# k'v and its product with q on halves of the TensorE array, all pieces of a batch in one slot

## The chip, the cores and the metric

One core of one Trainium2 chip. The metric is the device time of one execution, in microseconds (us). Runs of one kernel differ by a microsecond or two; so beside the times this text uses single executions taken by the profiler, stretch by stretch. PE is TensorE's matmul side, PEld its weight loads, DVE is VectorE, ACT ScalarE, POOL GpSimd, SP the engine that issues most transfers.

## The reference, cut to what matters

```python
def _attn_ref(q, k, v, g_norm):                    # (8 batches, 8 heads, 576 tokens, 64)
    kv = np.einsum('bhsd,bhse->bhde', k, v)        # 64 x 64 per head
    out = np.einsum('bhsd,bhde->bhse', q, kv)
    rms = np.sqrt(np.mean(out * out, axis=-1, keepdims=True) + 1e-06)
    return out / rms * g_norm
# then, on x = out as (4608 tokens, 512): gelu(x @ w_gate) * (x @ w_val) @ w_out,
# gated by sigmoid(x @ w_res), added to x
```

A head is 64 wide, half of the 128x128 array. Two heads side by side, a "pair", fill it. A batch has 4 x 128 tokens and a remainder of 64; the remainders of two batches share a tile of 128 rows.

Of the kernel before, what the change touches and what calls it, by code (L numbers as in the profile page):

```python
# [18 lines left out]
def kernel(  # L19
# [22 lines left out]
    NJ = 4  # L42
# [99 lines left out]
    def attn_begin(b):  # L142
        st[b] = {
            "qT": attnp.tile([P, NJ, NP, P], FP16, tag="qT", name="qT"),
            "kv2": attnp.tile([P, NP, P], FP16, tag="kv2", bufs=3, name="kv2"),
            "ss": attnp.tile([P, NJ + 1, H], FP32, tag="ss", name="ss"),
            "o": {},
        }
# [10 lines left out]
    def kv_steps(b, ps, pr):  # L159

        k16 = b16_t[b, "k"].rearrange("p j h d -> p j (h d)")
        v16 = b16_t[b, "v"]
        if b == 0:
            lasts = [[t[:, j].rearrange("p h d -> p (h d)") for t in first_last] for j in range(2)]
        else:
            lasts = [[t.rearrange("p h d -> p (h d)") for t in last_kv[b % 2]]]
        cs = slice(pr * P, (pr + 1) * P)
        for j in range(NJ):
            nc.tensor.matmul(  # L169
                ps,  # L170
                lhsT=k16[:, j, cs],
                rhs=v16[:, 2 * pr : 2 * pr + 2, j * D : (j + 1) * D],
                start=(j == 0),
                stop=False,
            )
        for i, (kl, vl) in enumerate(lasts):
            nc.tensor.matmul(ps, lhsT=kl[:, cs], rhs=vl[:, cs], start=False, stop=(i == len(lasts) - 1))  # L177

    def a_kv(b, lo, hi):
        if lo == 0:  # L180
            st[b]["kvp"] = pattn.tile([P, NP, P], FP32, tag="at", name="kvp")
        ps = st[b]["kvp"]
        for pr in range(lo, hi):
            kv_steps(b, ps[:, pr, :], pr)
        if hi == NP:
            nc.vector.tensor_tensor(
                out=st[b]["kv2"], in0=ps, in1=mask[:, None, :].to_broadcast([P, NP, P]), op=ALU.mult
            )

    def a_ss(b, j, ps):  # L190
        sq = attnp.tile([P, H, D], FP32, tag="sq", name="sq")
        nc.scalar.activation(out=sq, in_=ps, func=AF.Square)  # L192
        nc.vector.tensor_reduce(out=st[b]["ss"][:, j, :], in_=sq, op=ALU.add, axis=mybir.AxisListType.X)  # L193

    def a_o(b, j):
        s = st[b]
        ps = pattn.tile([P, C], FP32, tag="at", name="op")
        for pr in range(NP):
            nc.tensor.matmul(  # L199
                ps[:, pr * P : (pr + 1) * P], lhsT=s["qT"][:, j, pr, :], rhs=s["kv2"][:, pr, :], start=True, stop=True  # L200
            )
        a_ss(b, j, ps)
        s["o"][j] = ps

    def a_rem_o(b):
        ps = pattn.tile([P, C], FP32, tag="at", name="orp")
        for pr in range(NP):
            for e in range(2):
                nc.tensor.matmul(  # L209
                    ps[:, pr * P : (pr + 1) * P],  # L210
                    lhsT=qtr[e][:, pr, :],
                    rhs=st[2 * pair(b) + e]["kv2"][:, pr, :],
                    start=(e == 0),
                    stop=(e == 1),
                )
        o32 = attnp.tile([P, C], FP32, tag="o32", name="o32")
        nc.scalar.copy(out=o32, in_=ps)
        a_ss(b, NJ, ps)
        st[b]["o"][NJ] = o32
# [28 lines left out]
    def a_t(b, j):  # L248

        s = st[b]  # L250
        blk, jj = where(b, j)
        nc.vector.tensor_tensor(  # L252
            out=t_t[blk][:, jj, :].rearrange("p (h d) -> p h d", h=H),
# [591 lines left out]
```

## The kernel before: the parts that the change and the argument touch

The big matmuls of batch m (here "block m") run in slots of 8 matmuls of 512 columns, 1.73 us each. The attention of batch m+1 is put between the slots, in small pieces.

```python
def kv_steps(b, ps, pr):                  # k'v of one pair of heads, whole array
    ...
    cs = slice(pr * P, (pr + 1) * P)      # P = 128: two heads
    for j in range(NJ):                   # 4 token tiles, then the remainder
        nc.tensor.matmul(ps, lhsT=k16[:, j, cs], rhs=v16[:, 2*pr : 2*pr+2, j*D : (j+1)*D], ...)
    for i, (kl, vl) in enumerate(lasts):
        nc.tensor.matmul(ps, lhsT=kl[:, cs], rhs=vl[:, cs], ...)

def a_kv(b, lo, hi):
    ...                                   # two of the four blocks of a pair are of no use:
    nc.vector.tensor_tensor(out=st[b]["kv2"], in0=ps, in1=mask[...], op=ALU.mult)

def a_o(b, j):                            # product with q, one token tile
    ps = pattn.tile([P, C], FP32, tag="at", name="op")
    for pr in range(NP):
        nc.tensor.matmul(ps[:, pr*P : (pr+1)*P], lhsT=s["qT"][:, j, pr, :], rhs=s["kv2"][:, pr, :], ...)

def a_rem_o(b):                           # remainder rows of two batches
    ...  lhsT=qtr[e][:, pr, :]            # copies of qrT, each with the other batch's half zeroed

# in plan_attn(b): where the pieces stand (b == 2: k0, o0, n0 = 4, 6, 10; else 1, 3, 7)
at(m, k0, lambda: a_kv(b, 0, 2))          # half of k'v
at(m, k0 + 1, lambda: a_kv(b, 2, 4))      # the other half
at(m, o0, lambda: a_rem_o(b))             # if the batch has a remainder to do
for j in range(NJ):
    at(m, o0 + j, lambda j=j: a_o(b, j))  # four slots
```

## Time and profile before

| | before |
|---|---|
| time, median of 3 runs | 353.95 us |
| span of the profiled run | 352.1 us |
| PE busy | 343.4 us (98%) |
| DVE / ACT busy | 61% / 35% |

The page's groups by line and shape give the four groups of matmuls that the change touches. Columns: line, engine, operation, output and inputs, rows*columns of the array in use, shape of the moving tile, count; then busy time and mean ns of one; then idle time before them.

```profile
L169 PE MATMUL kvp<-v,k 128*128 128x128 f16 x128 | 11.0, 222 | 1.1 <-POOL v L535 0.8
L199 PE MATMUL op<-kv,qT 128*128 128x128 f16 x112 | 10.7, 219 | 0.0
L177 PE MATMUL kvp<-vl,kl 128*128 128x128 f16 x28 | 6.1, 219 | 0.0
L209 PE MATMUL orp<-kv,qtr 128*128 128x128 f16 x32 | 2.4, 219 | 0.0
```

They use all of the array (128*128), but half of each k'v result is thrown away by the mask, and half of what the product multiplies is zero. Do not read the cost off "mean ns": matmuls overlap in the pipeline, and what one costs is its distance to the next one's start, 0.0558 us here.

### The profile page before, as it was taken

What the parts mean: (1) busy time and instruction counts of PE and PEld (TensorE: products, weight loads), DVE (VectorE), ACT (ScalarE), POOL (GpSimd) and SP (SyncE); (2) the same over time, 40 slices, a digit from 0 to 9 for tenths busy, and PEclk for the clock granted to TensorE, in tenths of its full rate; (3) what the DMA queues carried; (4) which work ended last, traced back from release to release, by engine and by line L of the source; (5) the groups of instructions that cost most, each with busy time, mean ns of one, the idle gap of its engine ahead of it and who ended that gap; (6) DMA issues with size and microseconds to landing.
All of it is one profiled execution on the core that took longest, in us unless ns stands there. A gap on an engine that the chain in (4) does not pass through costs nothing.

```text
span 352.1 us, 5059 instructions
## 1 busy us (share of the span) xinstructions
PE 343.4 (98%) x1907; PEld 168.0 (48%) x1907; DVE 215.6 (61%) x434; ACT 124.9 (35%) x216; POOL 50.2 (14%) x79
## 2 busy tenths in 40 slices
PE   8799999999999999999999999999999999999995
PEld 3544554454454445444554455444544444444443
DVE  6855377869757765766478646855687433344433
ACT  3663534462254213522363125312642233223320
POOL 2782420150050005000320031000000000000000
PEclk9999999999999999999999999999999999999999
DMA  7999999697999079905691569037001500020013
GB/s 241 304 197 203 197 202 122 181 151 89 207 132 104 2 184 153 118 0 132 133 185 9 127 144 183 3 78 178 0 2 42 151 2 0 30 90 2 1 30 91
DMA packets 78507, 38.74 MB, mean 110 GB/s; under 512 B 42386, under 2 KB 74002, under 8 KB 78482
## 3 DMA queue, kind: packets, MB, share of 16 engines
q0 software_dynamic: 38752, 17.17, 38.9%
q1 hardware_dynamic: 39488, 21.11, 22.4%
q8 instruction: 15, 0.25, 0.3%
q10 hardware_dynamic: 242, 0.13, 0.1%
q14 instruction: 10, 0.08, 0.1%
HBM read 38.80 MB, written 9.44 MB: 137 GB/s over the span
## 4 chain that ended last, share of the span: by engine, by line
PE 91%; DMA 4%; DVE 3%; issue 0%; ACT 0%; SPq 0%; POOL 0%; DVEq 0%
PE gps L315 26%; PE vps L315 26%; PE fps L348 26%; PE rps L335 9%; PE kvp L169 2%; PE op L199 2%; DMA kf<-in_k_dram 2%; DMA vf<-in_v_dram 1%; DMA out_dram<-osb 1%; DVE t L594 1%; DVE ss L580 1%; PE orp L209 1%; PE kvp L177 0%; PE vps L620 0%; PE gps L620 0%
## 5 line engine op out<-in xcount | busy, mean ns | idle before, releaser
L304 DVE TENSOR_TENSOR hid<-ge,vps 128x512 f16<-128x512 f16 x108 | 73.3, 684 | 65.3 <-PE vps L315 58.5
L315 PE MATMUL gps<-xT,wg 128*128 128x512 f16 x424 | 108.8, 379 | 0.3 <-ACT xT L265 0.3
L315 PE MATMUL vps<-xT,wv 128*128 128x512 f16 x424 | 108.8, 379 | 0.0
L303 ACT ACTIVATE ge<-gps 128x512 f16<-128x512 f32 x108 | 64.4, 598 | 112.4 <-PE gps L315 103.3
L348 PE MATMUL fps<-wo,hid 128*128 128x512 f16 x420 | 96.7, 379 | 0.0
L315 PEld LDWEIGHTS <-wv 128*128 128x128 f16 x424 | 41.5, 98 | 50.0
L348 PEld LDWEIGHTS <-hid 128*128 128x128 f16 x420 | 40.8, 98 | 48.1
L315 PEld LDWEIGHTS <-wg 128*128 128x128 f16 x424 | 40.0, 98 | 41.8 <-issue 0.5
L354 DVE SCALAR_TENSOR_TENSOR pf<-th,fps 128x512 f32<-128x512 f32 x35 | 23.8, 687 | 47.8 <-PE fps L348 47.8
L344 ACT ACTIVATE th<-rps 128x512 f32<-128x512 f32 x36 | 21.5, 598 | 79.5 <-PE rps L335 79.5
L335 PE MATMUL rps<-wr,xT 128*128 128x512 f16 x144 | 36.5, 379 | 0.0
L193 DVE TENSOR_REDUCE ss<-sq 128x8 f32<-128x512 f32 x32 | 21.4, 683 | 6.3 <-ACT sq L192 4.6
L359 DVE SCALAR_TENSOR_TENSOR osb<-pf,t 128x512 f32<-128x512 f32 x35 | 24.2, 691 | 1.1
L335 PEld LDWEIGHTS <-xT 128*128 128x128 f16 x144 | 14.1, 98 | 17.0
L192 ACT ACTIVATE sq<-op 128x512 f32<-128x512 f32 x28 | 16.6, 598 | 9.7 <-PE op L199 9.0
L728 POOL COPY hold<-qT 1x1 f16<-1x1 f16 x5 | 0.9, 178 | 134.1 <-DMA qT<-q 134.1
L252 DVE TENSOR_TENSOR t<-op,ny 128x512 f16<-128x512 f32 x28 | 17.8, 680 | 0.1
L271 DVE TENSOR_TENSOR t<-t,g 128x512 f16<-128x512 f16 x36 | 13.3, 418 | 0.0
L169 PE MATMUL kvp<-v,k 128*128 128x128 f16 x128 | 11.0, 222 | 1.1 <-POOL v L535 0.8
L169 PEld LDWEIGHTS <-k 128*128 128x128 f16 x128 | 9.2, 100 | 5.1 <-issue 1.8
L199 PEld LDWEIGHTS <-qT 128*128 128x128 f16 x112 | 8.4, 98 | 5.5 <-issue 0.2
L199 PE MATMUL op<-kv,qT 128*128 128x128 f16 x112 | 10.7, 219 | 0.0
(107 smaller groups left out, 180.7 us busy)
## 6 DMA issues: line engine op xcount, KB each, us to landing
out_dram<-osb SPq DMA_DIRECT2D x32, 256.0 KB, 2.4
qraw<-in_q_dram POOLq DMA_DIRECT2D x7, 512.0 KB, 6.0
kraw<-in_k_dram POOLq DMA_DIRECT2D x7, 512.0 KB, 8.6
v<-in_v_dram POOLq DMA_DIRECT2D x7, 512.0 KB, 10.7
wg<-in_moe_w_gate_dram POOLq DMA_DIRECT2D x2, 512.0 KB, 8.2
wv<-in_moe_w_val_dram POOLq DMA_DIRECT2D x2, 512.0 KB, 8.9
wo<-in_moe_w_out_dram POOLq DMA_DIRECT2D x2, 512.0 KB, 14.5
out_dram<-osb SPq DMA_DIRECT2D x6, 128.0 KB, 2.3
```

The source lines that it names most:

```text
L169: nc.tensor.matmul(ps, lhsT=k16[:, j, cs], rhs=v16[:, 2 * pr : 2 * pr + 2, j * D : (j + 1) * D], start=(j == 0), stop=False,)
L193: nc.vector.tensor_reduce(out=st[b]["ss"][:, j, :], in_=sq, op=ALU.add, axis=mybir.AxisListType.X)
L199: nc.tensor.matmul(ps[:, pr * P : (pr + 1) * P], lhsT=s["qT"][:, j, pr, :], rhs=s["kv2"][:, pr, :], start=True, stop=True)
L252: nc.vector.tensor_tensor(out=t_t[blk][:, jj, :].rearrange("p (h d) -> p h d", h=H), in0=s["o"][j].rearrange("p (h d) -> p h d", h=H), in1 ...
L303: nc.scalar.activation(out=ge, in_=gps, func=AF.Gelu)
L304: nc.vector.tensor_tensor(out=hids[blk][:, f, :], in0=ge, in1=vps, op=ALU.mult)
L315: nc.tensor.matmul(ps[:, j0 * P : j1 * P], lhsT=w[:, cc, :], rhs=xT_t[blk][:, j0:j1, cc, :], start=(cc == 0 and j0 == 0), stop=(cc == NP - ...
L335: nc.tensor.matmul(rps, lhsT=xT_t[blk][:, j, cc, :], rhs=wr16[:, cc, :], start=(cc == 0), stop=(cc == NP - 1),)
L344: nc.scalar.activation(out=th, in_=rps, func=AF.Tanh, scale=0.5)
L348: nc.tensor.matmul(fps, lhsT=hids[blk][:, f, j * P : (j + 1) * P], rhs=wo16[:, f, :], start=(f == 0), stop=(f == NF - 1))
L354: nc.vector.scalar_tensor_tensor(out=pf, in0=th, scalar=1.0, in1=fps, op0=ALU.add, op1=ALU.mult)
L359: nc.vector.scalar_tensor_tensor(out=osb, in0=pf, scalar=0.5, in1=t_t[blk][:, j, :], op0=ALU.mult, op1=ALU.add)
```

## The change

The intent is to give the two heads of a pair a half of the array each. In k'v the halves are columns (64 of k as weights, output on 64 partitions), in the product they are rows (64 partitions of q' and of k'v). Neighbouring matmuls use different halves and can overlap. Since going from the whole array to halves and back costs time, all pieces of a batch stand in one slot: one visit for k'v, one for the product, one for the remainder. (A visit is a stretch of tiled matmuls between two whole-array ones.) The remainder uses quarters and goes a slot earlier; batch 0 keeps the old form. In batch 1 the normalisation and the first output transposes move a slot ahead as well. Core of the diff:

```diff
+    def a_kv(b):
+        ps = pattn.tile([P, NP, D], FP32, tag="at", name="kvp")
         for pr in range(NP):
+            for j in range(NJ + 1):
+                for e in range(2):
+                    h = 2 * pr + e
+                    nc.tensor.matmul(
+                        ps[halves(e), pr, :],
+                        lhsT=k16[:, j, h, :] if j < NJ else kl[:, h, :],
+                        rhs=v16[:, h, j * D : (j + 1) * D] if j < NJ else vl[:, h, :],
...
+        nc.vector.tensor_copy(out=st[b]["kv2"], in_=ps)
+    def a_o(b):
+        for jj in range(NJ // 2):
+            for e in range(2):
+                o[2 * jj + e] = pattn.tile([P, 2, NP, D], FP32, tag="at", name="op")
+            for j in range(2):
+                for pr in range(NP):
+                    for e in range(2):
+                        nc.tensor.matmul(
+                            o[2 * jj + e][:, j, pr, :],
+                            lhsT=st[b]["qT"][halves(e), 2 * jj + j, pr, :],
+                            rhs=kv_of(b, e, pr), ...
     def a_rem_o(b):
+                        ps[e][halves(i), pr, :],
+                        lhsT=qrT[halves(e), pr, halves(i)],
+                        rhs=kv_of(2 * pair(b) + i, e, pr), ...
...                                          # m_out_last, the last tile of the output
+        osb_all = finp.tile([P, C], FP32, tag="osb", bufs=3, name="osb")
-            osb = finp.tile([P, n], FP32, tag="osb", bufs=3, name="osb")
+            osb = osb_all[:, cs]
...                                          # opening: fillers that keep PE busy in waits
-    ... o0 rows8 vc2P ... t1 cols8 sq2 ...
+    ... o0 warm2 vc2P ... t1 warm1 sq2 ...
...                                          # plan of batch 1: x are the output transposes
-            2 * NF + 1: [x[0], x[1]],
-            2 * NF + 2: [x[2], x[3]],
+            2 * NF: [x[0], x[1]],
+            2 * NF + 1: [x[2]],
+            2 * NF + 2: [x[3]],
...                                          # plan of batches 2 to 7
-        at(m, k0, lambda: a_kv(b, 0, 2))
-        at(m, k0 + 1, lambda: a_kv(b, 2, 4))
+        at(m, k0, lambda: a_kv(b))
         if rem:
-            at(m, k0 + 1, lambda: rem_qT_copy(b))
-            at(m, o0, lambda: a_rem_o(b))
+            at(m, o0 - 1, lambda: a_rem_o(b))
+        at(m, o0, lambda: a_o(b))
```

More of the change, by code (lines that the diff above doesn't have):

```diff
@@ L144, in attn_begin @@
             "qT": attnp.tile([P, NJ, NP, P], FP16, tag="qT", name="qT"),
-            "kv2": attnp.tile([P, NP, P], FP16, tag="kv2", bufs=3, name="kv2"),
+            "kv2": (
+                attnp.tile([P, NP, D], FP16, tag="kv2", bufs=3, name="kv2")
+                if b > 0
+                else consts.tile([P, NP, P], FP16, name="kv0")
+            ),
             "ss": attnp.tile([P, NJ + 1, H], FP32, tag="ss", name="ss"),
@@ L157, in a_qT @@
         nc.scalar.copy(out=st[b]["qT"][:, 2 * jj : 2 * jj + 2, :, :], in_=ps)
-    def kv_steps(b, ps, pr):
-        k16 = b16_t[b, "k"].rearrange("p j h d -> p j (h d)")
-        v16 = b16_t[b, "v"]
-        if b == 0:
-            lasts = [[t[:, j].rearrange("p h d -> p (h d)") for t in first_last] for j in range(2)]
-        else:
-            lasts = [[t.rearrange("p h d -> p (h d)") for t in last_kv[b % 2]]]
-        cs = slice(pr * P, (pr + 1) * P)
-        for j in range(NJ):
-            nc.tensor.matmul(
-                ps,
-                lhsT=k16[:, j, cs],
-                rhs=v16[:, 2 * pr : 2 * pr + 2, j * D : (j + 1) * D],
-                start=(j == 0),
-                stop=False,
-            )
-        for i, (kl, vl) in enumerate(lasts):
-            nc.tensor.matmul(ps, lhsT=kl[:, cs], rhs=vl[:, cs], start=False, stop=(i == len(lasts) - 1))
@@ L179, in a_kv @@
-    def a_kv(b, lo, hi):
-        if lo == 0:
-            st[b]["kvp"] = pattn.tile([P, NP, P], FP32, tag="at", name="kvp")
-        ps = st[b]["kvp"]
-        for pr in range(lo, hi):
-            kv_steps(b, ps[:, pr, :], pr)
-        if hi == NP:
-            nc.vector.tensor_tensor(
-                out=st[b]["kv2"], in0=ps, in1=mask[:, None, :].to_broadcast([P, NP, P]), op=ALU.mult
-            )
-    def a_ss(b, j, ps):
-        sq = attnp.tile([P, H, D], FP32, tag="sq", name="sq")
-        nc.scalar.activation(out=sq, in_=ps, func=AF.Square)
-        nc.vector.tensor_reduce(out=st[b]["ss"][:, j, :], in_=sq, op=ALU.add, axis=mybir.AxisListType.X)
@@ L195, in a_o, with halves, kv_of @@
-    def a_o(b, j):
-        s = st[b]
-        ps = pattn.tile([P, C], FP32, tag="at", name="op")
-        for pr in range(NP):
-            nc.tensor.matmul(
-                ps[:, pr * P : (pr + 1) * P], lhsT=s["qT"][:, j, pr, :], rhs=s["kv2"][:, pr, :], start=True, stop=True
-            )
-        a_ss(b, j, ps)
-        s["o"][j] = ps
+    def halves(e):
+        return slice(e * D, (e + 1) * D)
+    def kv_of(b, e, pr):
+        kv2 = st[b]["kv2"]
+        return kv2[halves(e), pr, :] if b > 0 else kv2[halves(e), pr, halves(e)]
@@ new lines, in a_kv @@
+    def a_kv(b):
+        k16 = b16_t[b, "k"]
+        v16 = b16_t[b, "v"]
+        kl, vl = last_kv[b % 2]
+        ps = pattn.tile([P, NP, D], FP32, tag="at", name="kvp")
+        for pr in range(NP):
+            for j in range(NJ + 1):
[5 more added lines that the diff above has]
+                        rhs=v16[:, h, j * D : (j + 1) * D] if j < NJ else vl[:, h, :],
+                        start=(j == 0),
+                        stop=(j == NJ),
+                    )
+        nc.vector.tensor_copy(out=st[b]["kv2"], in_=ps)
@@ new lines, in a_o @@
+    def a_o(b):
+        o = st[b]["o"]
+        for jj in range(NJ // 2):
[7 more added lines that the diff above has]
+                            lhsT=st[b]["qT"][halves(e), 2 * jj + j, pr, :],
+                            rhs=kv_of(b, e, pr),
+                            start=True,
+                            stop=True,
+                        )
@@ new lines, in of_o, with a_ss @@
+    def of_o(ap, i):
+        jj, e = i // 2, i % 2
+        return ap[:, 2 * jj : 2 * jj + 2].rearrange("p j (r e) -> p j r e", e=2)[:, :, :, e]
+    def a_ss(b, i):
+        o, ss = st[b]["o"][i], st[b]["ss"]
+        sq = attnp.tile([P, 2, NP, D] if i < NJ else [P, H, D], FP32, tag="sq", name="sq")
+        src = o if i < NJ else o.rearrange("p (h d) -> p h d", h=H)
+        nc.scalar.activation(out=sq, in_=src, func=AF.Square)
+        out_ = of_o(ss, i) if i < NJ else ss[:, NJ, :]
+        nc.vector.tensor_reduce(out=out_, in_=sq, op=ALU.add, axis=mybir.AxisListType.X)
@@ L205, in a_rem_o @@
     def a_rem_o(b):
-        ps = pattn.tile([P, C], FP32, tag="at", name="orp")
+        qrT = st[b]["qrT"]
+        ps = [pattn.tile([P, NP, D], FP32, tag="at", name="orp") for _ in range(2)]
         for pr in range(NP):
             for e in range(2):
-                nc.tensor.matmul(
-                    ps[:, pr * P : (pr + 1) * P],
-                    lhsT=qtr[e][:, pr, :],
-                    rhs=st[2 * pair(b) + e]["kv2"][:, pr, :],
-                    start=(e == 0),
-                    stop=(e == 1),
-                )
@@ L216, in a_rem_o @@
-        o32 = attnp.tile([P, C], FP32, tag="o32", name="o32")
-        nc.scalar.copy(out=o32, in_=ps)
-        a_ss(b, NJ, ps)
-        st[b]["o"][NJ] = o32
+                for i in range(2):
+                    nc.tensor.matmul(
+                        ps[e][halves(i), pr, :],
+                        lhsT=qrT[halves(e), pr, halves(i)],
+                        rhs=kv_of(2 * pair(b) + i, e, pr),
+                        start=True,
+                        stop=True,
+                    )
@@ L221, in a_norm @@
+        st[b]["o"][NJ] = o32 = attnp.tile([P, C], FP32, tag="o32", name="o32")
+        for e in range(2):
+            nc.scalar.copy(out=o32.rearrange("p (r e d) -> p r e d", e=2, d=D)[:, :, e, :], in_=ps[e])
     def a_norm(b, j0, j1):
@@ L246, in where, with a_t @@
         return (b, j) if j < NJ else (B, pair(b))
-    def a_t(b, j):
-        s = st[b]
-        blk, jj = where(b, j)
-        nc.vector.tensor_tensor(
-            out=t_t[blk][:, jj, :].rearrange("p (h d) -> p h d", h=H),
-            in0=s["o"][j].rearrange("p (h d) -> p h d", h=H),
-            in1=s["rinv"][:, j, :, None].to_broadcast([P, H, D]),
-            op=ALU.mult,
-        )
+    def a_t(b, i):
+        o, rinv = st[b]["o"][i], st[b]["rinv"]
+        if i < NJ:
+            jj, e = i // 2, i % 2
+            t = t_t[b][:, 2 * jj : 2 * jj + 2, :].rearrange("p j (r e d) -> p j r e d", e=2, d=D)[:, :, :, e, :]
+            scale = of_o(rinv, i)[:, :, :, None].to_broadcast([P, 2, NP, D])
+        else:
+            t = t_t[B][:, pair(b), :].rearrange("p (h d) -> p h d", h=H)
+            o = o.rearrange("p (h d) -> p h d", h=H)
+            scale = rinv[:, NJ, :, None].to_broadcast([P, H, D])
+        nc.vector.tensor_tensor(out=t, in0=o, in1=scale, op=ALU.mult)
     def a_xT(b, j):
@@ L283, in d_rem_qT @@
         nc.sync.dma_start(out=st[b]["qrT"], in_=qr_t[pair(b)], transpose=True)
-    def rem_qT_copy(b):
-        nc.scalar.copy(out=qtr[0][:, :, 0:R], in_=st[b]["qrT"][:, :, 0:R])
-        nc.scalar.copy(out=qtr[1][:, :, R : 2 * R], in_=st[b]["qrT"][:, :, R : 2 * R])
     def d_xT(b, j0, j1):
@@ L482 @@
     nc.vector.tensor_copy(out=ident, in_=ident32)
-    qtr = [consts.tile([P, NP, P], FP16, name=f"qtr{i}") for i in range(2)]
     grow32 = consts.tile([1, 2, D], FP32, name="grow32")
@@ L488 @@
     nc.vector.tensor_copy(out=grow16, in_=grow[:, None, :].to_broadcast([1, H, D]))
-    for t in last_kv[0] + last_kv[1] + qtr:
-        nc.vector.memset(t if t.shape[1] == NP else t[R:P], 0.0)
+    for t in last_kv[0] + last_kv[1]:
+        nc.vector.memset(t[R:P], 0.0)
     idle = pmoe.tile([P, C], FP32, tag="mm", name="idle")
-    idle2 = pmoe.tile([P, C], FP32, tag="mm", name="idle2")
-    def keep_warm_tiles(n, rows):
-        for i in range(n):
-            for e in range(2):
-                at = slice(e * D, (e + 1) * D)
-                ps = (idle, idle2)[e]
-                if rows:
-                    nc.tensor.matmul(
-                        ps[:, i * D : (i + 1) * D], lhsT=zeros[at, 0:P], rhs=zeros[at, 0:D], start=True, stop=True
-                    )
-                else:
-                    nc.tensor.matmul(
-                        ps[at, i * D : (i + 1) * D], lhsT=zeros[:, 0:D], rhs=zeros[:, 0:D], start=True, stop=True
-                    )
     def keep_warm(n):
@@ L559, in f_kv @@
         first["kv", pr] = ps = pattn.tile([P, P], FP32, tag="at", name="kvp")
-        kv_steps(0, ps, pr)
+        k16 = b16_t[0, "k"].rearrange("p j h d -> p j (h d)")
+        hs, cs = of_pair(pr)
+        for j in range(NJ):
+            nc.tensor.matmul(
+                ps, lhsT=k16[:, j, cs], rhs=b16_t[0, "v"][:, hs, j * D : (j + 1) * D], start=(j == 0), stop=False
+            )
+        for j in range(2):
+            kl, vl = (t[:, j].rearrange("p h d -> p (h d)")[:, cs] for t in first_last)
+            nc.tensor.matmul(ps, lhsT=kl, rhs=vl, start=False, stop=(j == 1))
     def f_kv_out(pr):
@@ L631, in f_piece @@
         rest = word[len(name) :]
-        pr = int(rest[0]) if rest else 0
+        pr = int(rest[0])
         j0, j1 = {"a": (0, NJ // 2), "b": (NJ // 2, NJ)}.get(rest[1:2], (0, NJ))
@@ L640, in f_piece @@
             keep_warm(pr)
-        elif name in ("rows8", "cols8"):
-            keep_warm_tiles(8, name == "rows8")
         elif name == "wg":
@@ L680 @@
     qc1P qc0A qT1 qT0 kc1P kc0A qo0D warm3 lv0D lk0P qo1A warm3 vc1D vc0A kv1 qc2A kv0 kvo1 kvo0 o1 kc2P qT2
-    lk1P lv1D sq1 qo2D o0 rows8 vc2P sq0 rd1 kv2 qc3P rt1 kvo2 rd0 kc3A qT3 wg1 wv1 ri1 o2 rt0 t1 cols8 sq2 vc3D
+    lk1P lv1D sq1 qo2D o0 warm2 vc2P sq0 rd1 kv2 qc3P rt1 kvo2 rd0 kc3A qT3 wg1 wv1 ri1 o2 rt0 t1 warm1 sq2 vc3D
     rd2 qo3A xT1 kv3 wg2 wcg0P rt2 kvo3 ri0 ri2 warm2 o3 t2 xo1A wcg1P sq3a wcv0P sq3b g1 xT2 rd3a wcv1P rd3b
@@ L699, in attn_plan_1 @@
         b = 1
-        o = [lambda j=j: a_o(b, j) for j in range(NJ)]
+        ss = [lambda j=j: a_ss(b, j) for j in range(NJ)]
         t = [lambda j=j: a_t(b, j) for j in range(NJ)]
@@ L710, in attn_plan_1 @@
                 lambda: load_batch(b + 1),
-                lambda: a_kv(b, 0, NP),
+                lambda: a_kv(b),
             ],
-            NF + 4: [o[0], o[1]],
-            NF + 5: [o[2]],
-            NF + 6: [o[3]],
-            NF + 7: [lambda: a_norm(b, 0, NJ), t[0], t[1], t[2], t[3]],
-            2 * NF + 1: [x[0], x[1]],
-            2 * NF + 2: [x[2], x[3]],
+            NF + 4: [lambda: a_o(b), ss[0], ss[1]],
+            NF + 5: [ss[2], ss[3]],
+            NF + 6: [lambda: a_norm(b, 0, NJ), t[0], t[1], t[2], t[3]],
+            2 * NF: [x[0], x[1]],
+            2 * NF + 1: [x[2]],
+            2 * NF + 2: [x[3]],
         }
@@ L756, in plan_attn @@
         if rem:
-            at(m, k0 + 1, lambda: rem_qT_copy(b))
-            at(m, o0, lambda: a_rem_o(b))
+            at(m, o0 - 1, lambda: a_rem_o(b))
+            at(m, o0 + 2, lambda: a_ss(b, NJ))
+        at(m, o0, lambda: a_o(b))
         for j in range(NJ):
-            at(m, o0 + j, lambda j=j: a_o(b, j))
+            at(m, o0 + j // 2, lambda j=j: a_ss(b, j))
         at(m, n0, lambda: a_norm(b, 0, NJ + rem))
```

## The prediction

> **What bounds the kernel now.** I read the page's first part, then the chain that ended last, then what TensorE (PE) waited for, and then stretches of the timeline.
>
> ```profile
> PE 343.4 (98%) x1907; PEld 168.0 (48%) x1907; DVE 215.6 (61%) x434; ACT 124.9 (35%) x216; POOL 50.2 (14%) x79
> ...
> PE 91%; DMA 4%; DVE 3%; issue 0%; ACT 0%; SPq 0%; POOL 0%; DVEq 0%
> ...
> PE gps L315 <- ACT xT L265: 0.3, 1, 0.3
> ```
>
> PE is busy 98% of 352.1 us and is 91% of the chain. In the list of PE's waits all but the line shown lie in the first 17 us. So from there on the time is the sum of the spacings of PE's instructions, and a change is worth what it takes from that sum, less the waits it adds. VectorE (DVE, 61%) and ScalarE (ACT, 35%) have room.
>
> The change touches three groups on PE. By shape they are: k'v, 112 + 28 matmuls of 128x128 (lines 169 and 177, without the 16 and 8 of batch 0); its product with q, 112 (line 199); the remainder rows, 32 (line 209). What one costs is the spacing of starts: eight matmuls of 128 columns take 0.61 us of which the last one's own 0.219 is pipeline, so the spacing is (0.61 - 0.219)/7 = 0.0558 us.
>
> What a tiled matmul costs, this trace already holds, in fillers of the opening that use the halves by rows (line 504) and by columns (line 508). Columns: start, duration in us, engine, line, what.
>
> ```profile
> 11.06 0.39 PE L569 MATMUL op<-kv,qT 128*128 128x128 f16 x4
> 11.38 0.41 PE L504 MATMUL idle<-zeros 64*128 64x64 f16 x16
> ...
> 13.48 0.39 PE L569 MATMUL op<-kv,qT 128*128 128x128 f16 x4
> 13.80 0.44 PE L508 MATMUL idle<-zeros 128*64 128x64 f16 x16
> ...
> 11.38 0.29 PEld L504 LDWEIGHTS <-zeros 64*128 64x128 f16 x16
> 11.72 0.10 PEld L169 LDWEIGHTS <-k 128*128 128x128 f16 x1
> ```
>
> By rows: (0.41 - 0.190)/15 = 0.0147 us each, 0.0292 a pair (the single starts lie 3.5 ns and 26 ns apart in turn). By columns: 0.0317 a pair from the single starts. The way in: the last whole matmul starts at 11.06 + 0.39 - 0.219 = 11.23, the first tiled one at 11.38: 0.15 instead of 0.056, so 0.095 lost; by columns the same (13.65 to 13.80). The way out: the last tiled one starts at 11.60, the next whole weight load at 11.72: 0.12, some 0.1 lost.
>
> **What the Trainium skill says.** "TensorEngine Tiling (Array Packing)", Key Properties: changing the tiling mode drains TensorE, changing the tile doesn't. The trace agrees, with 0.095 us in and about 0.1 out. Its Theoretical Speedup gives two tiles up to 2x; here 0.0558/0.0292 = 1.9 by rows and 1.76 by columns. "TensorE: Matmul & The Clock Gate", Part 3, Measured speedup vs the span model, has about 4 ns for each further tile; 3.5 ns here. Nothing in this trace uses 64x64 tiles, which the remainder needs; I take that model for it. Gotcha 1 of the tiling page, that row tiles may not share a PSUM bank at once, is why the new code gives each half e its own tile.
>
> **The change, part by part** (from the start of the last other matmul before it to the start of the next one after it, so that switches are in).
> k'v: before 20 matmuls, 21 x 0.0558 = 1.17 us. After 20 pairs by columns: the filler's 8 pairs took 0.15 in, 0.25 in starts, 0.12 out = 0.52; 12 more pairs x 0.0317 = 0.38; 0.90. Gain 0.27.
> Product: before 17 x 0.0558 = 0.95; after 0.49 for the filler's 8 pairs, and 8 x 0.0292 = 0.23: 0.72. Gain 0.22.
> Seven batches: 7 x 0.49 = 3.45 us.
> Remainder, four times: before 9 x 0.0558 = 0.50. After 16 matmuls on four quarters; estimate, from the skill's model and the 26 ns spacing: four rounds of about 0.037 = 0.15, and 0.26 for the switches: 0.41. Gain 0.09, in all 0.36.
> Taken together 3.8 us on PE. Without the switches (3 visits x 0.2 us in a remainder batch, 2 in another: 18 in all, 3.6 us) it would be twice that. Putting all pieces of a batch into one slot is what keeps it at 18.
>
> Beside the path: the mask multiply of 128x512 (685 ns on DVE, 7 times) becomes a copy of half the elements; the eight ACT copies into qtr (0.4 us each) go, four remainder copies become eight halves. DVE gets two reductions in one slot and none in the next but one: a slot's DVE work is 3 x 0.6 = 1.8 us against about 1.73 + 0.72 us of PE in it. No PE wait follows.
>
> Three places where waits change. First, batch 1 enters block 1:
>
> ```profile
> 54.40 2.57 ACT L265 ACTIVATE xT<-xtp,gcol 128x512 f16<-128x512 f16 x4 [5.67 <-PE xtp L264]
> ...
> 55.28 0.61 PE L264 MATMUL xtp<-ident,t 128*128 128x128 f16 x8
> ...
> 55.73 1.03 PE L348 MATMUL fps<-wo,hid 128*128 128x512 f16 x4
> ...
> 57.02 0.81 PE L315 MATMUL gps<-xT,wg 128*128 128x512 f16 x3 [0.27 <-ACT xT L265]
> ```
>
> The last line should have started at 55.73 + 4 x 0.216 = 56.59; it waited 0.43 for two ACT copies. The change puts only one transpose before the last step (4 x 0.056 + 0.864 = 1.09 us of PE against 0.26 + 0.68 + 0.05 of latency and copy): nearly all of it goes, 0.36. The product's 0.08 wait for the mask (45.31 instead of 45.23) goes too. But the first two transposes move a slot ahead and may wait about 0.1 for t.
>
> Second, the end:
>
> ```profile
> 347.76 0.28 DVE L385 SCALAR_TENSOR_TENSOR pf<-th,fps 128x128 f32<-128x128 f32 x1
> 348.72 0.29 DVE L387 SCALAR_TENSOR_TENSOR osb<-pf,t 128x128 f32<-128x128 f32 x1 [0.68 <-DMA out_dram<-osb]
> ```
>
> The last piece waits 0.68 us for a buffer whose store has not landed. One buffer for the three pieces (osb_all) removes that. But the second stores are being issued until 348.45 (SP) and 348.74 (ACT), so the last issue moves from 349.04 to about 348.75: 0.3 to 0.4 us, I take 0.35.
>
> Third, the loss. The remainder product goes one slot earlier and reads the transposed q itself. For batch 2:
>
> ```profile
> 66.76 1.23 SPq L283 DMA_TRANSPOSE qrT<-qr  x1
> ...
> 68.81 1.03 PE L315 MATMUL gps<-xT,wg 128*128 128x512 f16 x4
> ...
> 69.19 0.41 ACT L286 COPY qtr<-qrT 128x256 f16<-128x256 f16 x1 [1.00 <-DMA qrT<-qr]
> ...
> 70.54 0.61 PE L209 MATMUL orp<-kv,qtr 128*128 128x128 f16 x8
> ```
>
> Today only ACT waits there, a microsecond. In the new order PE is there one slot (1.73 us) and half a k'v earlier: 70.54 - 1.73 - 0.56 + 0.28 (whole k'v in the slot before) = 68.53, with the switch 68.63. The transpose lands at 69.19 and hangs on work paced by PE in the same block, so it moves along. PE waits about 0.55 us. For batches 3, 5, 7 qrT lands two microseconds or more before it is wanted.
>
> Sum: 3.8 + 0.36 + 0.08 - 0.1 + 0.35 - 0.55 = 3.95 us. In the opening warm2 and warm1 replace fillers before waits of 0.8 and 0.7 us: nothing.
>
> **The rivals.** *Switches cost more.* If a drain behind 512-column matmuls cost 0.4 us a visit instead of 0.2, 18 visits would take the 3.6 us back: 353.6. For: the fillers had a wait behind them, so the way out is read from a weight load only, and they multiplied zeros with one and the same address. Against: both ways in measure 0.15 us to 10 ns.
> *PSUM turns into the bound.* All four product tiles are taken at once from a pool of four, with k'v and two remainder tiles just before. If the ACT copies or the DVE copy were late, PE would wait 0.3 to 0.5 us a batch: 351.5 to 352.5. For: the pool has no spare. Against: a slot of 1.73 us lies between, the copies need about 0.8 us after their matmuls, and ACT is at 35%.
> *All is hidden.* It isn't: nothing but PE is on the path after 17 us. The opposite rival, full overlap with free switches, would give 353.95 - 7.5 = 346.4, against the measured 0.095 us in.
>
> **Range and chances.** 353.95 - 3.95 = 350.0 us. An error of 0.05 us a visit is 0.9 us, the uncertain waits (0.55, 0.43, 0.35) some 0.6 together, and the runs of before spread 1.4 us: 348.7 to 351.8, more room above since an unseen wait is likelier than an unseen gain. 2% is 346.9, which needs nearly free switches: 4%. Slower by 2% would need 11 us of new waits: 2%. The rest, 94%, is within.
>
> **What would show it.** In the changed profile: the 280 k'v matmuls at about 0.032 us a pair, the 224 of the product at 0.029; about 0.1 us at each edge of a visit; PE waits for the transposed remainder once, in batch 2, near 0.55 us; no wait of osb for a store at the end; no 0.27 for xT at block 1's start. It is wrong if PE idles in every batch for PSUM tiles, or if pairs stand over 0.05 us apart (no overlap with true operands).

## The result, and the profile after

The changed kernel took 350.0 us (median of 4 runs, 349.87 to 355.88); the kernel before took 354.5 in the same rounds (353.59 to 355.12). The ratio is 0.987, interval 0.984 to 0.991: faster by 1.3%. A ratio is the mean time of one kernel's fast runs over that of the other's in the same rounds, so not quite the ratio of the medians. The run of 355.88 was slow (granted clock 0.983) and is left out of the ratio.

The page of the changed kernel, engines and chain:

```profile
PE 338.4 (97%) x2162; PEld 159.5 (46%) x2162; DVE 211.9 (61%) x432; ACT 122.0 (35%) x212; POOL 50.2 (14%) x79
...
PE 92%; DMA 4%; DVE 2%; SPq 0%; issue 0%; POOL 0%; ACT 0%; DVEq 0%
```

There are 255 matmuls more, and the span is 348.1 us instead of 352.1. PE is still the path. The same groups as above, in the changed kernel:

```profile
L182 PE MATMUL kvp<-v,k 128*64 128x64 f16 x224 | 5.5, 197 | 0.1
L182 PE MATMUL kvp<-vl,kl 128*64 128x64 f16 x56 | 4.7, 196 | 0.0
L200 PE MATMUL op<-kv,qT 64*128 64x64 f16 x224 | 4.5, 191 | 0.0
...
L228 PE MATMUL orp<-kv,qrT 64*64 64x64 f16 x64 | 1.3, 198 | 0.6 <-DMA qrT<-qr 0.6
```

128*64, 64*128 and 64*64 are the three kinds of tiles. Twice as many matmuls (280 for 140, 224 for 112), at about the same latency of 0.19 to 0.20 us each; what fell is the spacing. It shows in the timeline of batch 3 (start, duration, engine, line, what, count):

```profile
96.38 0.59 PE L331 MATMUL vps<-xT,wv 128*128 128x512 f16 x2
96.91 0.32 PE L182 MATMUL kvp<-v,k 128*64 128x64 f16 x8
97.05 0.20 PE L182 MATMUL kvp<-vl,kl 128*64 128x64 f16 x2
...
97.53 0.20 PE L182 MATMUL kvp<-vl,kl 128*64 128x64 f16 x2
97.66 1.04 PE L331 MATMUL gps<-xT,wg 128*128 128x512 f16 x4
98.53 1.03 PE L331 MATMUL vps<-xT,wv 128*128 128x512 f16 x4
99.49 0.32 PE L228 MATMUL orp<-kv,qrT 64*64 64x64 f16 x16
99.74 1.04 PE L331 MATMUL gps<-xT,wg 128*128 128x512 f16 x4
...
101.57 0.64 PE L200 MATMUL op<-kv,qT 64*128 64x64 f16 x32
```

The 40 matmuls of k'v start between 96.91 and 97.53: a pair every 0.0317 us. The 32 of the product take (0.64 - 0.19)/31 = 0.0145 us each. Before k'v there is a gap: the second of the two 512-column matmuls starts at 96.38 + 0.59 - 0.379 = 96.59, without a switch the next would start 0.216 later, at 96.81, and it started at 96.91. After it, the last starts at 97.53 and the next whole one at 97.66. These edges, 0.093 to 0.096 us in and 0.122 to 0.129 out, are alike in all eighteen visits but two that also waited for data.

The three places at which the prediction looked for waits. Batch 2's remainder:

```profile
65.81 1.23 SPq L303 DMA_TRANSPOSE qrT<-qr  x1
...
68.25 0.32 PE L228 MATMUL orp<-kv,qrT 64*64 64x64 f16 x16 [0.59 <-DMA qrT<-qr]
```

PE, not ACT, now waits for the transpose. The list counts 0.59 us, from the modelled end of the matmul before; by starts it is 0.66, for that matmul started at 67.28 and 67.28 + 0.216 + 0.095 = 67.59. The entry to block 1:

```profile
52.50 0.62 PE L284 MATMUL xtp<-ident,t 128*128 128x128 f16 x8
...
54.90 0.39 PE L284 MATMUL xtp<-ident,t 128*128 128x128 f16 x4
55.13 1.03 PE L364 MATMUL fps<-wo,hid 128*128 128x512 f16 x4
56.07 1.02 PE L331 MATMUL gps<-xT,wg 128*128 128x512 f16 x4
```

55.13 + 4 x 0.216 = 55.99: the wait for xT is 0.08 instead of 0.43. But the first transposes stood 0.19 us waiting for t. And the end:

```profile
343.75 2.05 ACTq L409 DMA_DIRECT2D out_dram<-osb  x3
...
344.16 0.28 DVE L402 SCALAR_TENSOR_TENSOR pf<-th,fps 128x128 f32<-128x128 f32 x1
344.47 0.29 DVE L404 SCALAR_TENSOR_TENSOR osb<-pf,t 128x128 f32<-128x128 f32 x1
```

The last addition no longer waits for a store. From the last matmul's start to the last instruction it is 4.25 us instead of 4.61.

### The profile page after: what moved, and what is told of

Same layout as the page of the kernel before. It is cut to its first block, busy times and chain, and to the rows that moved or that the text cites. A ratio compares the mean times of both kernels' runs of the same rounds, so it can differ in the third digit from the quotient of the medians.

```text
span 348.1 us, 5543 instructions
## 1 busy us (share of the span) xinstructions
PE 338.4 (97%) x2162; PEld 159.5 (46%) x2162; DVE 211.9 (61%) x432; ACT 122.0 (35%) x212; POOL 50.2 (14%) x79
## 2 busy tenths in 40 slices
DMA packets 78508, 38.77 MB, mean 111 GB/s; under 512 B 42386, under 2 KB 74002, under 8 KB 78482
## 4 chain that ended last, share of the span: by engine, by line
PE 92%; DMA 4%; DVE 2%; SPq 0%; issue 0%; POOL 0%; ACT 0%; DVEq 0%
PE gps L331 27%; PE fps L364 26%; PE vps L331 26%; PE rps L351 9%; DMA vf<-in_v_dram 2%; DMA kf<-in_k_dram 1%; PE kvp L182 1%; PE op L200 1%; DMA qrT<-qr 1%; DVE t L601 1%; DVE ss L587 1%; PE vps L627 0%; PE fps L394 0%; PE gps L627 0%; PE xtp L284 0%; PE orp L228 0%
## 5 line engine op out<-in xcount | busy, mean ns | idle before, releaser
L219 DVE TENSOR_REDUCE ss<-sq 128x8 f32<-128x512 f32 x32 | 20.6, 679 | 2.9 <-ACT sq L217 2.7
L217 ACT ACTIVATE sq<-op 128x512 f32<-128x512 f32 x28 | 15.3, 597 | 4.5 <-PE op L200 4.2
L512 PE MATMUL idle<-zeros 128*128 128x512 f16 x19 | 7.2, 505 | 1.2 <-DVE zeros L485 1.2
L99 POOL DMA_DIRECT2D qraw<-in_q_dram x7 | 6.3, 895 | 5.9 <-DVE q L107 4.0
L101 POOL DMA_DIRECT2D v<-in_v_dram x7 | 6.3, 904 | 0.0
L100 POOL DMA_DIRECT2D kraw<-in_k_dram x7 | 6.3, 899 | 0.1
```

The lines of the kernel that those rows point to most:

```text
L217: nc.scalar.activation(out=sq, in_=src, func=AF.Square)
L219: nc.vector.tensor_reduce(out=out_, in_=sq, op=ALU.add, axis=mybir.AxisListType.X)
```

## The experiments

Two ways of comparing are used. One is time. The other is the profile of each run, cut into stretches at PE's big groups of matmuls (gate and value / residual and output, alternating). In all profiles the stretches without attention are equal to 0.01 us (13.81 and 20.72 us), so a change of a few hundredths shows. What varies between two profiles of one kernel is the opening, everything up to the first residual matmul of block 0. So the table gives the opening, and the rest of the span from there on. The twelve runs all gave right results.

| kernel | opening | rest of span | rest, against the changed kernel | median of runs, us | runs with clock under 0.997 |
|---|---|---|---|---|---|
| before | 38.90 | 313.16 | +3.73 | 353.7 to 354.5 by call | see below |
| changed | 38.66 | 309.43 | 0 | 350.0 | 1 of 4 |
| e0 changed again | 38.85 | 309.45 | +0.02 | 350.88 | 4 of 6 |
| e2 remainder's transpose first | 38.77 | 308.74 | -0.69 | 349.43 | 2 of 6 |
| e8 and batch 1's transposes moved | 39.43 | 308.75 | -0.68 | 349.78 | 2 of 6 |
| e4 product in four visits | 39.01 | 313.24 | +3.81 | 354.28 | 2 of 4 |
| e5 halves in turn | 40.23 | 313.63 | +4.20 | 355.54 | 2 of 4 |
| e3 k'v whole | 38.51 | 311.06 | +1.63 | 352.46 | 2 of 4 |
| e6 product whole | 39.50 | 310.88 | +1.45 | 352.25 | 3 of 4 |
| e1 before, one output buffer | 38.73 | 312.75 | (-0.41 against before) | 353.19 | 1 of 4 |
| e9 more fillers | 38.94 | 309.61 | +0.18 | 350.29 | 0 of 5 |
| e10 old fillers | 41.04 | 310.92 | +1.49 | 353.12 | 5 of 6 |
| e7 before again | 39.51 | 313.16 | (0.00 against before) | 354.45 | 1 of 1 |
| e11 best | 38.46 | 308.67 | -0.76 | 349.31 | 0 of 6 |

**e0, the changed kernel again.** No edit.

> The changed kernel once more, on the chip that runs the next three, for comparison. All theories: 350.0 us within 0.3, ratio to the kernel before 0.986 to 0.990. The opening (up to the first matmul of slot 2 of block 0, at 21.39 us in the changed kernel's profile and 21.64 before) tells whether its quarter of a microsecond is the change's (then 21.4 again) or the input transfers' (then anything from 21.2 to 21.8).

350.1 to 352.4 us, median 350.88, ratio 0.992: both outside what was expected. Four of its six runs had a mean granted clock of 0.995, which goes some of the way; one at full clock took 350.86 too. After the opening it is the first profile to 0.02 us. The opening was 38.85, not 38.66: the quarter of a microsecond of the first profile was not the change's.

**e4, the product in four visits.**

```diff
-        at(m, o0, lambda: a_o(b))
+        for j in range(NJ):
+            at(m, o0 + j, lambda j=j: a_o(b, j))      # 8 matmuls each, batches 2 to 7
```

> From batch 2 on the product of a batch is cut into four visits of 8 tiled matmuls in four slots, as the kernel before placed it, in place of one of 32: 18 visits more, the same matmuls. Theory (each visit costs a drain in and out, 0.10 + 0.11 us on PE): 18 x 0.21 = 3.8 us, so 353.8, which is nearly the kernel before; in the profile the visits show 0.095 us in and 0.12 us out each. Rival (the switches are mostly hidden behind the 512-column matmuls and one slot each is tidiness): 350.0 to 350.8.

3.81 us more, 3.8 expected; by time 354.28, as slow as the kernel before. Batch 3's visits in this run:

```profile
101.82 0.81 PE L336 MATMUL vps<-xT,wv 128*128 128x512 f16 x3
102.56 0.29 PE L205 MATMUL op<-kv,qT 64*128 64x64 f16 x8
102.79 1.04 PE L336 MATMUL gps<-xT,wg 128*128 128x512 f16 x4
```

From 101.82 + 0.81 - 0.379 + 0.216 = 102.47, when the next big matmul would have started, to 102.79 it is 0.32 us for 8 tiled matmuls, of which 0.10 are their starts. The four whole matmuls that do the same work in the kernel before take 4 x 0.0558 = 0.22. So tiles in the old places would have lost time: 4 x 0.32 = 1.28 us a batch for the product against 0.89 before. The one slot is not tidiness, it is what makes the change pay. The rival falls.

**e5, the halves in turn.**

```diff
-            for j in range(NJ + 1):
-                for e in range(2):          # k'v; the product likewise
+        for e in range(2):
+            for pr in range(NP):
+                for j in range(NJ + 1):
```

> The same tiled matmuls, but all of one half first and then all of the other, so that neighbours never use different halves. Theory (the gain is two halves working at once): a matmul of 64 columns alone is spaced about 0.027 us, 40 of them 1.1 us instead of 0.63 and 32 of them 0.88 instead of 0.45: 0.9 us a batch more, 7 batches 6.3 us, 356.3, slower than the kernel before. Rival (the gain is from moving half the columns and loading half the weights, the order does not matter): 350.0.

4.2 us more, so slower than the kernel before by time too, 355.54. The rival falls, but the size was expected at 6.3. In k'v it is near what was expected: 0.53 us a batch more for 0.47, a matmul every 0.0296 us. The product lost only 0.17 instead of 0.43. In this run's timeline:

```profile
104.42 0.81 PE L200 MATMUL op<-kv,qT 64*128 64x64 f16 x32
```

(0.81 - 0.19)/31 = 0.020 us each, less than the 0.029 at which one half alone goes. In this edit the product changes halves after every eight matmuls, k'v only once after twenty. The single starts of the product lie 29 ns apart at first and then alternate 18 and 12 ns: the eight of one half overlap with the next eight of the other. The semaphores in the packed trace confirm it: the matmul that opens the second eight with a wait starts at 104.554, the one that closes the first eight by raising a semaphore only at 104.634. Taken apart like this, each eight goes at 29 to 30 ns after a first step of 38 to 40, and the next eight begins when five of the one before have started. In batch 2 most of what was lost went into the wait for the transpose, which shrank by 0.48: block 1 grew by only 0.2.

**e3, k'v on the whole array again.**

```diff
-                        ps[halves(e), pr, :],
-                        lhsT=k16[:, j, h, :] if j < NJ else kl[:, h, :],
+                    ps[:, pr, :],
+                    lhsT=k16[:, j, cs] if j < NJ else kl[:, cs],
...
-        nc.vector.tensor_copy(out=st[b]["kv2"], in_=ps)
+        nc.vector.tensor_tensor(out=st[b]["kv2"], in0=ps, in1=mask[...], op=ALU.mult)
```

> The changed kernel with k'v of batches 1 to 7 on the whole array again, in one slot, with the mask; product and remainder stay tiled. Theory (the parts add up on PE): 0.26 us a batch is lost and 0.37 in batch 2, where the switch lay inside another wait: 1.9 us, 351.9. Rival (the dropped mask multiply and the smaller copy on VectorE matter as well): over 352.5, with PE waits at the remainder product for the masked result.

1.63 more. Batches 1 and 3 to 7 lost 0.26 each, as expected, and the tail was 0.07 longer; batch 2 lost nothing, where 0.37 was expected. Its wait shrank instead:

```profile
68.37 0.32 PE L228 MATMUL orp<-kv,qrT 64*64 64x64 f16 x16 [0.23 <-DMA qrT<-qr]
```

So in the changed kernel whatever PE saves ahead of that wait is waited away. No wait for the masked result appeared, so the rival falls.

**e6, the product on the whole array again**, from a block-diagonal k'v in buffers zeroed once.

```diff
+            for pr in range(NP):
+                nc.tensor.matmul(o[j][:, pr * P : (pr + 1) * P],
+                                 lhsT=st[b]["qT"][:, j, pr, :], rhs=st[b]["kv2"][:, pr, :], ...)
```

> The changed kernel with the product of batches 1 to 7 on the whole array again, all 16 matmuls of a batch in one slot, from a block-diagonal k'v whose off-diagonal blocks are zeroed once; k'v and remainder stay tiled. Theory: 0.21 to 0.22 us a batch is lost: 1.5 us, 351.5. VectorE makes two copies of k'v instead of one, about 0.3 us a batch, off the path. Rival (the product's share is larger, since rows need no wait for other halves): 352.5 or more.

1.45 more (0.17 in batch 1, then 0.21 to 0.22 a batch), 1.5 expected. The times of this kernel and the last scatter over 2 us and would not have told 1.5 from 2.5.

**e1, the kernel before with one output buffer.**

```diff
+        osb_all = finp.tile([P, C], FP32, tag="osb", bufs=3, name="osb")
-            osb = finp.tile([P, n], FP32, tag="osb", bufs=3, name="osb")
+            osb = osb_all[:, cs]
```

> The kernel before with one part of the change: one output buffer for the three last pieces. Theory: the 0.68 us wait of the last addition for a store goes, but the last store is then held by the issue of the one before: 0.36 us off (last matmul to end 4.61 to 4.25 us), 353.6, ratio 0.999. Rival (the wait's whole 0.68 us comes off): 353.3, last matmul to end 3.95 us. The time will not tell these apart, the profile will.

0.41 less: last matmul to end 4.20 instead of 4.61. The 0.68 us wait went, and 0.27 of it was given back, as the theory said, to the issue of the stores: in this run the ACT queue issues its second store from 347.82 to 348.56, and only then the third.

**e2, batch 2's remainder transposed first.**

```diff
-            begin.append(lambda: d_rem_qT(b))
+            begin.insert(2 if b == 2 else 3, lambda: d_rem_qT(b))
```

> Only edit: for batch 2 the transpose of the remainder rows is issued before that of q. Theory (PE waited for a late transpose that it alone could not hide): the wait of 0.59 us before the remainder product of batch 2 goes, nothing else moves, PE then needs q's transpose 1.2 us later than before and gets it in time: 0.6 us off, 349.4. Rival (the wait only moves to q's transpose, which now lands 1.2 us later): a new wait at batch 2's product, 350.0 or above.

0.69 less, of which block 1 has 0.66; median 349.43. Batch 2's remainder product, in this run, without a wait:

```profile
66.73 1.03 PE L331 MATMUL vps<-xT,wv 128*128 128x512 f16 x4
67.69 0.32 PE L228 MATMUL orp<-kv,qrT 64*64 64x64 f16 x16
```

The rival, a new wait for q's transpose, did not show here. It did later (e9).

**e8, and batch 1's first three output transposes one slot later.**

```diff
-            2 * NF: [x[0], x[1]],
-            2 * NF + 1: [x[2]],
+            2 * NF + 1: [x[0], x[1], x[2]],
```

> The edit of the run above, and batch 1's first three output transposes together one slot later. Theory: the 0.59 us wait goes as above; the 0.19 us in which PE waited for the normalised values of batch 1 goes too, and ScalarE's four copies still end within 0.1 us of block 1's start: 0.8 us off, 349.2, span 347.3. Rival (ScalarE's copies then end too late and PE waits for the last one at block 1's start): no better than the run above, 349.4 to 349.8.

Nothing beyond e2. The 0.19 us wait for t went, and PE waited 0.21 for xT at block 1's start instead (56.84 against 55.77 + 4 x 0.216 = 56.63): the rival was right.

**e9, more fillers in the opening.** In the profiles of e5 and e6 a stretch of 3.4 us in the opening ran at half clock. The edit is e2's, with

```diff
-    ... o0 warm2 vc2P ... t1 warm1 sq2 ...
+    ... o0 warm3 warm3 vc2P ... t1 warm2 warm2 sq2 ...
-            2 * NF + 1: [x[2]],
-            2 * NF + 2: [x[3]],
+            2 * NF + 1: [x[2], x[3]],
```

> A candidate: the remainder transpose of batch 2 first, batch 1's last two output transposes together one slot earlier, and the fillers of the opening's two long PE waits raised from 2 and 1 matmuls of 512 columns to 6 and 4 (0.86 and 0.65 us more, inside waits of 1.3 and 0.9 us). Theory (runs with a mean granted clock near 0.995 have lost one 3.4 us stretch at half clock to those two waits, and cost about a microsecond): all or nearly all runs at 0.997 or more, median 349.3, fastest 349.2, where 18 of 38 runs with the changed kernel's opening had 0.995 or less. Rival (the slow stretch does not hang on these waits): two or three runs of six near 0.995 again.

The clock came out as the theory said: all five runs at 0.997 or more, and within half a microsecond of each other. The time did not: 350.29, for batch 2 had a wait again, now for q's transpose:

```profile
70.80 0.64 PE L200 MATMUL op<-kv,qT 64*128 64x64 f16 x32 [0.86 <-DMA qT<-q]
```

**e10, the changed kernel with the old fillers**, tiled pairs again instead of warm2 and warm1.

```diff
-    ... o0 warm2 vc2P ... t1 warm1 sq2 ...
+    ... o0 rows8 vc2P ... t1 cols8 sq2 ...
```

> The changed kernel with the opening's old fillers (8 tiled pairs by rows, 8 by columns) in place of 2 and 1 whole matmuls. Theory (the fillers lie inside waits for data): fast runs at 350.0 to 350.3 as the changed kernel, opening 38.6 to 38.9 us to the first matmul after it in a run at full clock, and as many runs near a clock of 0.995 as it, two or three of six. Rival (the new fillers are part of the gain or of the slow stretches): fast runs over 350.5, or none near 0.995.

353.12 us, far from the 350.0 expected: the theory missed, and the rival's sign came, for even the one run at a clock of 0.998 took 351.32. The profile shows two causes. The profiled run lost a stretch at half clock, from 15.9 to 19.3 us, and by their mean clocks four of the other five lost one too. And the wait in batch 2 had grown:

```profile
PE orp L228 <- DMA qrT<-qr: 2.1, 1, 2.1
```

Why does filler in the first 20 us change a wait at 70 us? The transposes were issued at the same place as in all runs (7.80 us after block 1's start), but landed 1.5 us later. I looked for other packets on the transfer engines in that time and found one: a fetch of 16 KB on the instruction queue. In fourteen profiles (times in us from block 1's start; landing is when POOL, which waits for the second of the two, goes on):

```
runs                                       fetch starts    took        transposes landed
before, e7, e1, e3                         none near       -           12.25 to 12.27
changed, e0, e4, e5, e6                    13.1 to 14.0    0.98-1.43   12.25 to 12.30
e2, e8                                     13.23, 13.10    0.96, 1.81  12.99, 13.00
e10                                        11.26           0.96        13.77
e9, e11                                    12.42, 12.43    0.89, 0.93  14.54, 14.60
```

(e2, e8, e9 and e11 issue the two in the other order, so the second is q's and lands later.) Where the fetch began before the usual landing, and only there, the landing is 1.5 to 1.6 us late. The single packets agree: in e9 the fetch ends at 13.30, and from 13.31 to 14.34 nine packets of the transposes' queue follow one after the other, when that queue's others are done; in e10 24 packets of that queue took 0.9 to 1.4 us, where in the eleven runs without a collision none took over 0.16. I take the fetch as the cause. I take its moment to depend on the number of instructions before it: the old fillers are 58 more than the new, e9's are 14 more. No run moved the fetch alone, so this stands on fourteen profiles and not on an edit of its own.

**e7, the kernel before again.** No edit.

> The kernel before, profiled once more. Theory (the opening varies with the input transfers, the rest is fixed): from the opening's end on every stretch as long as in the first profile to 0.02 us, tail 4.6 us; the opening itself anywhere from 38.5 to 39.5 us, or longer by one to two us if a stretch at half clock falls in it. Rival: the opening is 38.90 again, so the changed kernel's 38.66 is its own gain.

The rest of the span is 313.16 again, to the hundredth. The opening was 39.51 with a stretch at half clock. The clock column (the one before the last two) of this run's stretches shows it:

```profile
8.00:12.00 4.00, 2.35 (x42) 1.78 (x41) 1.95 (x6) 2.32 (x4) 1.52 (x3) 1.00 1.11 313
12.00:16.00 4.00, 2.88 (x41) 2.29 (x41) 3.32 (x9) 2.67 (x7) 3.95 (x7) 0.76 1.13 364
16.00:20.00 4.00, 3.27 (x21) 1.81 (x20) 3.31 (x10) 2.29 (x6) 4.00 (x7) 0.81 1.36 199
```

**e11, the best.** e9, with batch 2's remainder product and product one slot later, so that a late landing is covered wherever the fetch falls.

```diff
-            k0, o0, n0 = 4, 6, 10
+            k0, o0, n0 = 4, 7, 10
```

> The candidate before, with batch 2's remainder product and product one slot later (the square sums still end before its normalisation). Theory (in the candidate before and in the run with old fillers one 16 KB instruction fetch lay on a DMA engine while batch 2's transposes ran and made them land 1.5 us late, so PE waited; a slot of slack covers a fetch at any place): no PE wait in batch 2, block 1 shorter by 0.93 us than the candidate's 23.75 (22.8 us), block 2 on unchanged; all runs at a clock of 0.997 or more; median 349.4, fastest 349.1. Rival (moving the product by a slot only moves the wait, to PSUM tiles or to the normalisation): 350.0 or more.

349.31 us median (348.91 to 350.53), ratio 0.986. Block 1 is 22.82 us instead of 23.75, all six runs have a clock of 0.998 or more. The landing was late in this run too, and no wait came of it. What PE waited for, first three lines:

```profile
PE idle L512 <- DVE zeros L485: 1.2, 1, 1.2
PE vps L627 <- DVE t L601: 0.6, 1, 0.6
PE gps L627 <- POOL wg L654: 0.2, 1, 0.2
```

It is 0.76 us ahead of the changed kernel after the opening, and its clock is steadier. One of its runs took 350.53 at a clock of 0.998; nothing says why.

## Why the prediction was right, point by point

The predicted time was 350.0 us and the measured one 350.0. Part of that is luck, and the terms show which part. (In the rounds of the result the kernel before had a median of 354.5, so the drop is 4.5 there, 3.97 between the two profiles, 3.95 as predicted.)

- **PE's spacings bound the time.** Right. Each experiment that put spacings back got them back in full, except ahead of batch 2's wait. The list of PE's waits left one out: before batch 2's k'v PE stood 0.30 us in the kernel before (65.96 instead of 64.79 + 4 x 0.216 = 65.65). It stands under the weight loads, as a wait for DVE's k. In the changed kernel that visit's way in falls into this wait, which saves another 0.09.
- **k'v gains 0.27 a batch, the product 0.22, the remainder 0.09.** From spacings before (20, 16 and 8 x 0.0558) and measured after: 1.116 to 0.847, 0.893 to 0.669, 0.446 to 0.344, so 0.27, 0.22, 0.10. e3 and e6 take the first two back alone: 0.26 and 0.21 to 0.22. (In the prediction 7 x 0.49 is 3.43, not 3.45, and the whole sum 3.94; this changes nothing.) A hundredth a visit was missing in the sum: the second big matmul after a visit stands 0.226 us from the first instead of 0.216, 0.18 us for eighteen visits.
- **A visit costs about 0.2 us in switches.** Right, and e4 is the test: eighteen visits more cost 3.81 us, 0.21 each. The rival of dearer switches falls, and so does the one of free ones.
- **Two halves at once are the gain.** The prediction took it from fillers that multiplied zeros. e5 shows it with real operands.
- **Block 1's entry: 0.36 + 0.08 - 0.1.** The 0.43 us wait fell to 0.08 (0.35), the 0.08 went, but the wait for t was 0.19 instead of 0.1.
- **The end: 0.35.** 0.36 in the changed kernel, 0.41 in e1, for the reason given.
- **Batch 2's wait: 0.55.** 0.59 by the list, 0.66 by starts, and 0.66 is what e2 took out of block 1. What the wait does was judged too mildly: the prediction booked all gains of batch 2 and then took the wait off. That sum is near enough, but the wait is for a fixed moment, so it takes back whatever is gained ahead of it. Block 1 is 23.48 us, against 23.49 before: batch 2 gained nothing.
- **The opening: nothing.** The first profile had 0.24 us there, e0 only 0.05. Without the openings the two profiles differ by 3.73 us, where 3.95 were predicted: the hundredth a visit, the wait for t and 0.11 more of batch 2's wait cost more than foreseen, the 0.09 above and roundings gave some back, and the luck of one opening made up for the rest.
- **"Fillers before waits: nothing."** This is the statement that fell, and the larger luck. e10 is the changed kernel without this one edit, and it took 353.12 us, ratio 0.997 (the kernel before had 353.93 in that round): some 3 us of the median hung on the term that was booked as nothing. 1.5 us of it is the wait in batch 2, since with the old fillers the instruction fetch meets the transposes; the rest is the opening, with half-clock stretches in five of six runs. The other terms, read after the opening and without this wait, stay as they are. As for the stretches: 18 of 38 runs with the changed kernel's fillers had a mean clock under 0.997 (it and e0, e2, e3, e4, e5, e6, e8; one of them is the slow run of the result), 27 of 52 with the old ones (runs of before, with e1, e7 and e10), none of 11 with e9's fillers. By these clocks, runs without a stretch average 349.4 us in e2, those with it 350.9. So more fillers are worth a microsecond or more in such a run. That is likely also why the ratios of one and the same kernel ran from 0.987 to 0.992.
- **No PSUM bound.** Right: in the changed kernel's list of PE's waits there is none for a PSUM tile after the opening.

What stays open: the remainder's tiles and the new order at block 1's entry, which no experiment undid, so that their terms are read from the traces alone; whether the old fillers make half-clock stretches more frequent than the new ones (5 of 6 in e10 against 18 of 38, but 4 of 12 runs of the kernel before in one call and 9 of 11 in another); and the fetch, which no edit moved by itself.

## What to carry to other kernels

Tiling the array costs once a visit and pays with each matmul: here a visit cost 0.21 us and a pair of tiled matmuls saved 0.024 to 0.027. By these numbers, an estimate, a visit on halves with fewer than eight or nine pairs loses; collect the pieces first. A wait for a transfer that lands at a fixed moment takes back all that is gained ahead of it, so look for it before you count a gain, and give it a slot of slack rather than the exact place, since an instruction fetch can delay the landing. When run times scatter by more than the effect, compare stretches of the profile: those without the change must agree to the hundredth, and then those with it can be read.

## What the Trainium skill lacked or had wrong

- "TensorEngine Tiling (Array Packing)", Key Properties, says that changing the mode drains TensorE, without a number. Here: 0.093 to 0.096 us in, 0.122 to 0.129 from the last tiled start to the next whole one, 0.01 on the matmul after; 0.21 us a visit. Eight tiled matmuls then cost 0.32 us where four whole ones cost 0.22.
- The same page, Instruction Overhead, gives each matmul about 60 cycles on TRN2 and no gain below that size. Here 64-column matmuls on one half stand 29.6 ns apart, two halves give a pair every 29 (rows) or 31.7 ns (columns), and quarters 16 matmuls within 0.126 us of starts. That section does not say whether tiles share this overhead; by these spacings they do not.
- "TensorE: Matmul & The Clock Gate", Part 3, says that weight loads overlap with matmuls in flight only when the row group differs. Column halves share their rows, and here the weight loads and matmuls of a pair still start about 3 ns apart. It also calls the starts strictly in order, without reordering. In e5 the first matmul of the second eight starts 80 ns before the last of the first eight: between halves the order of starts was not that of the kernel's text.
- The same page, Part 1, describes the window of about 3.4 us after which an idle PE falls to half clock. The traces agree: the half-clock stretches were 3.4 us. That PE need not be idle throughout is not plain there: in e7, PE was busy 1.91 of the 3.41 us right before the stretch (10.69 to 14.10), and in e5, e6 and e10 1.66 to 1.78. The edge is not sharp in busy time: in the changed kernel 1.80 of such a window (10.68 to 14.09) brought no stretch.
- No page that I found says that an instruction fetch can hold up the kernel's own transfers; "Runtime: NRT & Kernel Launch", Instruction fetch mechanics, would be the place. Here a fetch is 16 KB and takes 0.9 to 1.8 us, and in the three runs where one fell among batch 2's transposes, these landed 1.5 to 1.6 us late.
